# Batch-aligned token groups, merged transposes and merged stores in a pooled-attention and tanh-shrink kernel

## The chip, the cores and the metric

The kernel runs on one NeuronCore of one Trainium2 chip. The metric is the device time of one execution in microseconds (us), the median of several runs. The engines are named as in the profile: PE (TensorE, matmuls), PEld (its weight loads, which overlap PE), DVE (VectorE), ACT (ScalarE), POOL (GpSimd) and SP (SyncE, which here only issues DMAs). An instruction queue with a q behind its name (SPq) is the engine's sequencer. Matmul results go to PSUM, eight banks of 512 fp32 per partition; everything else that is on the core lies in SBUF, 128 partitions wide. A DMA moves data on up to 16 DMA engines.

## The reference: what is computed

Inputs are q, k and v of shape (8 batches, 8 heads, 576 tokens, 64), and two weights, w_in (512 x 2048) and w_out (2048 x 512). All are fp32.

```python
k_p = k.reshape(B, H, 72, 8, D).mean(axis=3)      # keys and values pooled by 8 tokens
v_p = v.reshape(B, H, 72, 8, D).mean(axis=3)
scores = scale * q @ k_p^T ; attn = softmax(scores)
attn_out = attn @ v_p                             # (8, 8, 576, 64)
x = attn_out.transpose(0, 2, 1, 3).reshape(4608, 512)
h = x @ w_in
out = (h - tanh(h)) @ w_out                       # (4608, 512)
```

## The kernel before

**Groups of tokens.** The second half (h, then the product with w_out) works on 9 groups of 512 tokens. A batch has 576 tokens, so in the kernel before group g holds tokens 512 g to 512 g + 511 of the running numbering, and its edges drift through the batches: group 1 is the last 64 tokens of batch 0 and 448 of batch 1, group 8 is the last 512 of batch 7. Within a batch the first 512 tokens are stored with token 4 p + j at partition p of block j (j = 0 to 3), so that one partition reads a contiguous stretch; the last 64 tokens (QT) form a short block.

**x.** Attention output is made in blocks of 128 tokens by av (L441): av_mms (L391) issues six matmuls for a block, whose weights are 128 columns of E (the exponentials) and which stream 130 columns of VB (the pooled values and a column for the denominator). DVE takes the reciprocal (rden, L433) and multiplies (x_sb, L434). The fifth block of a batch takes the last 128 tokens, S - 128 to S, of which 64 are used. x_sb then has to be transposed into xT, with features on partitions: by PE against an identity and an ACT copy for batches 0 and 1 (x0_turn L856, x_pe_transpose L468), by a DMA transpose on SP for batches 2 to 7 (x_dma_transpose L457). xT is one ring of 3 x 512 token columns; a block that crosses the ring's end takes two transposes. Blocks that the next group does not need are put on the list `late`, and their transposes are issued when the next group starts its products. x_sb has five buffers.

**One group** (loop at L964) has two stages. In the h stage, 64 matmuls of 512 columns (h_mms, L555) fill pairs of PSUM banks; ACT makes the tanh (TS, L570) and DVE the difference (Gt, L571). In the product stage, the multiplication with w_out is done as seven products of half matrices, 14 units of 8 x 2 matmuls of 256 columns (product, L610), with sums on DVE and copies on ACT in between (after_product, L652). The attention of batch g + 1 is threaded into the units of group g: scores (L359) at units 0 to 4, and av at units 6, 7, 8, 9 and 11. A score tile t of 0 to 3 holds one pair of heads; t = 4 holds what is left of all pairs, as four matmuls with 32-column weights each. Scores of batches 2 to 7 are computed in two halves of 288 columns, each with its own exponential on ACT; batches 0 and 1 use 512 columns and a joint tail of 64 (scores_wide L374, scores_tail L383). Groups 7 and 8 have no attention threaded in.

**Order of the work.** The schedule is written out by hand; each engine runs its instructions in program order, and the framework adds the semaphores. SP issues, per group: the k transpose of the next batch, five q transposes (L205), the loads of the batch after that (k, v, q), and the x transposes. POOL issues the stores of the group before (store_tile, L633) at the start of a group, then copies kT into KB (k_place), and pools k and v of a later batch in the product stage. PSUM banks are handed out in turn (Banks, L74).

**Group 0 and group 1's attention** stand before the loop: group 0's h and product are threaded with batch 1's attention (L921 to L959, units u = 0 to 15 of four matmuls each), with its k transpose at u = 2, q transposes at u = 3 to 5, av at u = 9 to 13 and the x transposes two units later.

**Stores.** out_segments (L484) cuts a tile of 128 tokens where it crosses a batch or a block, so a tile takes one to three DMAs. The last group is stored in halves of 256 columns as its products come out (store L628, called at L667, L668, L1020, and the loop at L1025), by SP, POOL and ACT. The issue lines are L631, L635 and L1026:

```python
for r0, r1, dst in out_segments(g * TG + th * HT + tt * 128, 128):
    engs[tt].dma_start(out=dst[:, c0:c1], in_=O[r0:r1, 2 * th + tt, c0:c1])
```

Of the kernel before, what the change touches and what calls it, by code (L numbers as in the profile page):

```python
# [19 lines left out]
NHP = H // 2  # L20
# [3 lines left out]
T = B * S  # L24
NFB = DM // 128
# [9 lines left out]
RING = 3 * TG  # L35
# [7 lines left out]
def kernel(  # L43
# [54 lines left out]
    xT = const.tile([128, NFB, RING], BF16, name="xT")  # L98
# [100 lines left out]
    def q_dma_transpose(b, j0=0, j1=R + 1):  # L199
        if j0 == 0:  # L200
            qTs[b] = work.tile([128, NHP, S], BF16, name="qT", tag="qT")
        qT = qTs[b]
        for j in range(j0, j1):
            rows = 128 if j < R else QT
            nc.sync.dma_start_transpose(  # L205
                out=qT[:, :, j * 128 : j * 128 + rows],
                in_=q_bf[:rows, j, :, :].rearrange("p h d -> p (h d)"),
            )

    def q_pe_transpose(b, hps, eng=None):  # L210
        if b not in qTs:
            qTs[b] = work.tile([128, NHP, S], BF16, name="qT", tag="qT")
        qT = qTs[b]
        for hp in hps:
            ps = ps_any([128, QA], FP32, "qT_ps")
            for j in range(R):
                nc.tensor.matmul(
                    ps[:, j * 128 : (j + 1) * 128],
                    lhsT=q_bf[:, j, 2 * hp : 2 * hp + 2, :].rearrange("p h d -> p (h d)"),
                    rhs=ident[:, :],  # L220
                    start=True,
                    stop=True,
                )
            evac(qT[:, hp, 0:QA], ps[:, :], eng)

    def q_pe_tail(b):
# [9 lines left out]
        evac(qTs[b][:, :, QA:S], ps[:, :, :])  # L236
# [109 lines left out]
    def score_mms(b, t, dst, c0, c1, pairs=range(NM)):  # L346
        for m in pairs if t == NM else (t,):
# [6 lines left out]
                rhs=qTs[b][:, m, c0:c1],  # L354
                start=True,
                stop=True,
            )

    def scores(b, t):  # L359
        if t == 0:  # L360
            E_tiles[b] = work.tile([128, NT, S], BF16, name="E", tag="E", bufs=1)
        E = E_tiles[b]
        hs = S // 2
        pss = []
        for half in range(2):
            ps = ps_b1([128, hs], FP32, "s_ps")
            score_mms(b, t, ps[:, :], half * hs, (half + 1) * hs)
            pss.append(ps)
        for half, ps in enumerate(pss):
            nc.scalar.activation(  # L370
                out=E[:, t, half * hs : (half + 1) * hs], in_=ps[:, :], func=ACT.Exp, scale=SCALE
            )

    def scores_wide(b, ts):  # L374
# [3 lines left out]
        for t in ts:  # L378
            ps = ps_any([128, QA], FP32, "s_ps")
            score_mms(b, t, ps[:, :], 0, QA)  # L380
            nc.scalar.activation(out=E[:, t, 0:QA], in_=ps[:, :], func=ACT.Exp, scale=SCALE)

    def scores_tail(b):  # L383
        ps = ps_any([128, NT, QT], FP32, "s_ps")
        for t in range(NT):
            score_mms(b, t, ps[:, t, :], QA, S)
# [4 lines left out]
    def av_mms(b, blk, half, ps):  # L391
        E = E_tiles[b]
        vb = VB[b % 2]
        c0 = blk * 128 if blk < 4 else S - 128
        for n in range(3):
# [6 lines left out]
                lhsT=E[:, t, c0 : c0 + 128],  # L402
# [7 lines left out]

    def av_half(b, blk, half, x_sb, alloc):
        ps = alloc([128, 4, D1], FP32, "x_ps")
        av_mms(b, blk, half, ps)
        rden = work.tile([128, 4, 1], FP32, name="rden", tag="rden", bufs=4)
        nc.vector.reciprocal(out=rden[:, :, :], in_=ps[:, :, D:D1])
# [3 lines left out]
            in1=rden[:, :, :].to_broadcast([128, 4, D]),  # L419
# [3 lines left out]
    def new_x():  # L423
        return work.tile([128, 2, 4, D], BF16, name="x_sb", tag="x_sb", bufs=5)

    def av_both(b, blk, x_sb):
        b0 = ps_a.ids[ps_a.n % len(ps_a.ids)]
        ps_a.n += 2
        ps = PS[:, b0 : b0 + 2, 0 : 4 * D1].rearrange("p k (h d) -> p k h d", d=D1)
        for half in range(2):  # L430
            av_mms(b, blk, half, ps[:, half, :, :])
        rden = work.tile([128, 2, 4, 1], FP32, name="rden2", tag="rden2")
        nc.vector.reciprocal(out=rden[:, :, :, :], in_=ps[:, :, :, D:D1])  # L433
# [3 lines left out]
            in1=rden[:, :, :, :].to_broadcast([128, 2, 4, D]),  # L437
# [3 lines left out]
    def av(b, blk, alloc, by_dma):  # L441
        x_sb = new_x()
        if by_dma:
# [4 lines left out]
        if by_dma:  # L448
            if b * S + blk * 128 < (b + 1) * TG:
                x_dma_transpose(b, blk, x_sb)  # L450
            else:
                late.append((b, blk, x_sb))
        return x_sb

    late = []

    def x_dma_transpose(b, blk, x_sb):  # L457
        p0 = 0 if blk < 4 else 64
        pos = (b * S + blk * 128) % RING
        p1 = min(128, p0 + RING - pos)  # L460
        for r0, r1, c in ((p0, p1, pos), (p1, 128, 0)):
            if r1 > r0:
                nc.sync.dma_start_transpose(
                    out=xT[:, :, c : c + r1 - r0],
                    in_=x_sb[r0:r1, :, :, :].rearrange("p a h d -> p (a h d)"),
                )

    def x_pe_transpose(b, blk, x_sb, fbs=(0, 4)):  # L468
        p0 = 0 if blk < 4 else 64
        pos = b * S + blk * 128  # L470
        f0, f1 = fbs
        xf = x_sb.rearrange("p a h d -> p (a h d)")
        ps = ps_any([128, f1 - f0, 128], FP32, "xT_ps")
        for fb in range(f0, f1):
            nc.tensor.matmul(
                ps[:, fb - f0, p0:128],
                lhsT=xf[:, fb * 128 : (fb + 1) * 128],
                rhs=ident[:, p0:128],
# [3 lines left out]
        nc.scalar.copy(out=xT[:, f0:f1, pos : pos + 128 - p0], in_=ps[:, :, p0:128])  # L482

    def out_segments(c0, nrows):  # L484
        segs = []
        r = 0
        while r < nrows:
            c = c0 + r
            bb = c // S
            i = c % S  # L490
            if i < QA:
                j = i // 128
                p0 = i % 128
                ln = min(128 - p0, nrows - r, QA - i)
                dst = out[bb * S : bb * S + QA, :].rearrange("(p j) m -> p j m", j=R)[
                    p0 : p0 + ln, j, :
                ]
            else:
                ln = min(S - i, nrows - r)
                dst = out[bb * S + i : bb * S + i + ln, :]  # L500
            segs.append((r, r + ln, dst))
            r += ln
        return segs
# [3 lines left out]
    def mlp_h_mms(g, i, f0, f1, pool=None):  # L507
        tok0 = g * TG
        if f0 == 0:
            h_tiles[i] = ps_h.tile([128, TG]) if pool is None else pool  # L510
        for fb in range(f0, f1):
# [3 lines left out]
                rhs=xT[:, fb, tok0 : tok0 + TG],  # L515
# [18 lines left out]
    def mlp_o(g, tb, i0, i1, gts, pool=None):  # L534
# [12 lines left out]
        if i1 == NHID:  # L547
# [4 lines left out]
            for r0, r1, dst in out_segments(g * TG + tb * 128, 128):  # L552
                nc.sync.dma_start(out=dst, in_=o_sb[r0:r1, :])

    def h_mms(g, i, dst):  # L555
        c0 = (g * TG) % RING
        for fb in range(NFB):
# [3 lines left out]
                rhs=xT[:, fb, c0 : c0 + TG],  # L561
# [66 lines left out]
    def store(g, th, engs, c0, c1):  # L628
        for tt in range(2):
            for r0, r1, dst in out_segments(g * TG + th * HT + tt * 128, 128):  # L630
                engs[tt].dma_start(out=dst[:, c0:c1], in_=O[r0:r1, 2 * th + tt, c0:c1])  # L631

    def store_tile(g, tb):  # L633
        for r0, r1, dst in out_segments(g * TG + tb * 128, 128):
            nc.gpsimd.dma_start(out=dst, in_=O[r0:r1, tb, :])  # L635
# [16 lines left out]
    def after_product(g, n):  # L652
# [11 lines left out]
        if n == 3:  # L664
            nc.vector.tensor_tensor(out=O[:, 0:2, HD:DM], in0=m4, in1=chain(g, C2), op=ALU.subtract)
            if g == NG - 1:
                store(g, 1, (nc.sync, nc.sync), 0, HD)  # L667
                store(g, 0, (nc.sync, nc.sync), HD, DM)  # L668
# [14 lines left out]
    zeros = xT[:, NFB - 1, RING - 512 : RING]  # L683
# [172 lines left out]
    def x0_turn(blks, half, b0, eng):  # L856
        n = len(blks)
        ps = bank(b0, [128, 2, n, 128])
        for i, blk in enumerate(blks):
# [8 lines left out]
        c = blks[0] * 128  # L868
        eng(
            out=xT[:, 2 * half : 2 * half + 2, c : c + n * 128],  # L870
            in_=ps.rearrange("p f i c -> p f (i c)"),
# [34 lines left out]
    for i in range(5, NHID):  # L906
# [5 lines left out]
        if i == 11:  # L912
            x4 = av(0, 4, ps_any, False)
        if i == 13:
            x_pe_transpose(0, 4, x4)
# [5 lines left out]
    for u in range(16):  # L921
        qd, tb = u // 4, u % 4
# [136 lines left out]
```

## Time and profile before

| what | value |
|---|---|
| median of 3 runs | 294.2 us (294.19 to 294.36) |
| the profiled execution's own time | 293.78 us |
| its span, first to last instruction | 292.1 us |
| granted TensorE clock | 0.997 |
| PE busy | 279.8 us (96% of the span) |
| DVE, ACT, POOL busy | 222.5, 153.4, 135.9 us |
| DMA moved | 49.84 MB, mean 171 GB/s |
| end of the last matmul | 286.4 us |

How to read it: times are from the start of the span. A row of a group of instructions names the line, the engine, the operation and what it writes and reads (out<-in). A row of waits says who waited for whom, and how long in total, how often, and at most. A stretch row gives its length, the busy time of PE, PEld, DVE, ACT and POOL with their numbers of instructions, the granted clock, the share of time that the 16 DMA engines were busy, and what they moved in GB/s. The chain that ended last is followed back from the last instruction; each piece has its start and its length. For a DMA the issue is on the issuing engine, and "to landing" runs from the issue until its semaphore tells that all data has arrived.

### The profile page before, as it was taken

How to read it: one execution, taken by the hardware profiler on the slowest of the kernel's cores; microseconds unless marked ns; L12 is line 12 of the kernel's file. 1: busy time of each engine (PE TensorE's matmuls, PEld its weight loads, DVE VectorE, ACT ScalarE, POOL GpSimd, SP SyncE). 2: the span in 40 equal slices, each digit the busy share in tenths (PEclk: the TensorE clock that was granted, in tenths of full speed). 3: DMA queues.
4: the chain of work that ended last, by engine and by line, in shares of the span. 5: the costliest groups of instructions: out<-in, count | busy, mean ns of one | idle time of the engine just before them, and what ended most of it. 6: DMA issues, size and time to landing. Idle time of an engine off the chain costs nothing.

```text
span 292.1 us, 5384 instructions
## 1 busy us (share of the span) xinstructions
PE 279.8 (96%) x2040; PEld 179.0 (61%) x2040; DVE 222.5 (76%) x348; ACT 153.4 (53%) x243; POOL 135.9 (47%) x160
## 2 busy tenths in 40 slices
PE   7999989999999998999999989999999999999992
PEld 3454445445874686458845874489448944874681
DVE  5659666689986996599859975998599849927971
ACT  4747586586438642765186516660866056225510
POOL 8600818990199429911994199408950040030001
PEclk9999999999999999999999999999999999999998
DMA  7999999938936999599959994998392360021023
GB/s 253 228 212 281 304 204 336 308 77 249 247 72 105 285 319 114 134 241 314 97 102 264 323 120 89 258 333 118 79 190 44 61 167 2 0 79 67 0 57 90
DMA packets 64810, 49.84 MB, mean 171 GB/s; under 512 B 40048, under 2 KB 53744, under 8 KB 64784
## 3 DMA queue, kind: packets, MB, share of 16 engines
q1 hardware_dynamic: 54816, 35.40, 51.6%
q0 software_dynamic: 7312, 12.19, 18.8%
q10 hardware_dynamic: 2656, 1.90, 2.3%
q8 instruction: 16, 0.26, 0.4%
q14 instruction: 10, 0.08, 0.1%
HBM read 36.70 MB, written 9.44 MB: 158 GB/s over the span
## 4 chain that ended last, share of the span: by engine, by line
PE 74%; DMA 12%; DVE 5%; POOL 4%; issue 1%; ACT 1%; SPq 0%; POOLq 0%; DVEq 0%; ACTq 0%
PE PS L558 34%; PE PS L614 29%; DMA w1b<-in_moe_w_in_dram 4%; PE PS L540 4%; DMA xT<-x_sb 4%; DMA k_raw<-in_k_dram 4%; PE PS L398 3%; PE PS L351 3%; DVE Gt L571 2%; POOL k_raw L248 1%; ACT q_bf L192 1%; DVE P L579 1%; DVE m L671 1%; POOL k_raw L255 1%; POOL kd L258 1%
## 5 line engine op out<-in xcount | busy, mean ns | idle before, releaser
L558 PE MATMUL PS<-xT,w1b 128*128 128x512 bf16 x512 | 111.8, 379 | 2.9 <-DVE rden L433 1.3
L571 DVE TENSOR_TENSOR Gt<-PS,TS 128x1024 bf16<-128x1024 f32 x56 | 68.3, 1220 | 31.2 <-ACT TS L570 31.2
L558 PEld LDWEIGHTS <-w1b 128*128 128x128 f16 x512 | 49.7, 98 | 62.4 <-issue 2.8
L570 ACT ACTIVATE TS<-PS 128x1024 f32<-128x1024 f32 x56 | 57.3, 1024 | 33.2 <-PE PS L558 29.2
L248 POOL TENSOR_TENSOR k_raw<-k_raw 128x512 f32<-128x512 f32 (+2 forms) x13 | 21.1, 1638 | 74.2 <-DVE rden L433 44.2
L635 POOL DMA_DIRECT2D out_dram<-O x44 | 23.7, 547 | 40.0 <-DVE O L673 22.3
L614 PE MATMUL PS<-w2s,Dg 128*128 128x256 f16 x256 | 30.2, 273 | 0.0
L614 PEld LDWEIGHTS <-Gt 128*128 128x128 bf16 x256 | 24.4, 98 | 5.6 <-DVE Gt L576 0.5
L614 PEld LDWEIGHTS <-P 128*128 128x128 bf16 x256 | 24.6, 98 | 4.7 <-issue 1.4
L614 PEld LDWEIGHTS <-Dg 128*128 128x128 bf16 x256 | 24.5, 98 | 2.6
L370 ACT ACTIVATE E<-PS 128x288 bf16<-128x288 f32 x60 | 21.4, 410 | 8.1 <-PE PS L351 7.8
L434 DVE TENSOR_TENSOR x_sb<-PS,rden 128x512 bf16<-128x512 f32 x30 | 20.7, 691 | 5.9 <-DMA xT<-x_sb 5.0
L579 DVE TENSOR_TENSOR P<-Gt 128x1024 bf16<-128x1024 bf16 x32 | 22.2, 694 | 0.6
L398 PE MATMUL PS<-VB,E 128*128 128x130 bf16 x240 | 20.2, 220 | 0.1
L670 ACT COPY m<-PS 128x512 f32<-128x512 f32 x8 | 4.7, 586 | 29.5 <-PE PS L614 29.5
L589 DVE TENSOR_TENSOR Dg<-Gt 128x1024 bf16<-128x1024 bf16 x32 | 19.9, 682 | 0.0
L269 POOL TENSOR_TENSOR v_raw<-v_raw 128x512 f32<-128x512 f32 (+1 forms) x12 | 19.7, 1657 | 0.0
L398 PEld LDWEIGHTS <-E 128*128 128x128 bf16 x240 | 16.8, 98 | 1.9 <-issue 0.4
L351 PE MATMUL PS<-qT,KB 128*128 128x288 bf16 (+5 forms) x128 | 17.0, 289 | 0.1
L1019 ACT COPY O<-PS 128x512 f32<-128x512 f32 x7 | 4.1, 585 | 24.5 <-PE PS L614 24.5
L614 PE MATMUL PS<-w2s,Gt 128*128 128x256 f16 x128 | 16.7, 273 | 0.2 <-DVE Gt L576 0.2
L614 PE MATMUL PS<-w2s,P 128*128 128x256 f16 x128 | 16.3, 273 | 0.0
(112 smaller groups left out, 389.6 us busy)
## 6 DMA issues: line engine op xcount, KB each, us to landing
k_raw<-in_k_dram SPq DMA_DIRECT2D x7, 1024.0 KB, 9.1
q_raw<-in_q_dram SPq DMA_DIRECT2D x7, 1024.0 KB, 11.3
v_raw<-in_v_dram SPq DMA_DIRECT2D x7, 1024.0 KB, 11.3
out_dram<-O POOLq DMA_DIRECT2D x32, 128.0 KB, 3.8
out_dram<-O POOLq DMA_DIRECT2D x12, 256.0 KB, 3.5
w1b<-in_moe_w_in_dram POOLq DMA_DIRECT2D x4, 512.0 KB, 13.9
w2b<-in_moe_w_out_dram POOLq DMA_DIRECT2D x4, 512.0 KB, 17.3
out_dram<-O SPq DMA_DIRECT2D x4, 256.0 KB, 4.6
```

What stands on the lines that cost most here:

```text
L248: first = eng.tensor_tensor(out=r[:, ta:tb, 0:4, :], in0=r[:, ta:tb, 0:4, :], in1=r[:, ta:tb, 4:8, :], op=ALU.add)
L351: nc.tensor.matmul(dst[p : p + w], lhsT=KB[b % 2][:, o : o + w], rhs=qTs[b][:, m, c0:c1], start=True, stop=True,)
L370: nc.scalar.activation(out=E[:, t, half * hs : (half + 1) * hs], in_=ps[:, :], func=ACT.Exp, scale=SCALE)
L398: nc.tensor.matmul(ps[:, 2 * n : 2 * n + 2, :].rearrange("p h d -> p (h d)") if n < 2 else ps.rearrange("p (a s) d -> p a s d", s=2)[:, :, ...
L434: nc.vector.tensor_tensor(out=x_sb[:, :, :, :], in0=ps[:, :, :, 0:D], in1=rden[:, :, :, :].to_broadcast([128, 2, 4, D]), op=ALU.mult,)
L558: nc.tensor.matmul(dst, lhsT=w1b[:, fb, i * 128 : (i + 1) * 128], rhs=xT[:, fb, c0 : c0 + TG], start=(fb == 0), stop=(fb == NFB - 1),)
L570: nc.scalar.activation(out=t2, in_=PS[:, b0 : b0 + 2, :], func=ACT.Tanh)
L571: nc.vector.tensor_sub(out=Gt[:, p, :, :], in0=PS[:, b0 : b0 + 2, :], in1=t2)
L579: nc.vector.tensor_tensor(out=P[:, a:b, :], in0=Gt[:, a:b, 0, :], in1=Gt[:, a:b, 1, :], op=ALU.add)
L589: return nc.vector.tensor_tensor(out=Dg[:, a:b, :, :], in0=Gt[:, a:b, :, 0:HT], in1=Gt[:, a:b, :, HT:TG], op=ALU.subtract,)
L614: nc.tensor.matmul(part(g, bk, tt), lhsT=lhs(k, slice(tt * 128, (tt + 1) * 128)), rhs=rhs[:, k, :], start=(first and k == 0 and (tt == 0 o ...
L635: nc.gpsimd.dma_start(out=dst, in_=O[r0:r1, tb, :])
```

## The change

Group g of 0 to 7 becomes the first 512 tokens of batch g, and group 8 becomes the last 64 tokens of all eight batches. What follows from it:

- x lies in 128-token blocks: two buffers xT[0] and xT[1] of four blocks, one for even and one for odd batches, and xT_last for group 8, whose tile t holds the tails of batches 2 t and 2 t + 1. h_mms streams x[:, :, fb, :], four runs of 128 columns.
- x_sb holds a pair of blocks, and one DMA transpose turns a pair (128 x 1024); the tail takes a third one of 64 rows. The transposes of blocks 2 and 3 are issued behind av of block 3. The list `late` goes. The tails of batches 0 and 1 are turned by DMA, not by PE.
- q is laid out alike: qT in blocks plus a separate tail qt, with three DMA transposes per batch instead of five.
- Scores of batches 2 to 7 use scores_wide and scores_tail; av moves one unit earlier, to units 5, 6, 7, 8 and 10. The fifth block computes 64 rows, with 64-column weights.
- Stores: one DMA per half group (two tiles); for group 8 one per tile, whose destination is two runs of 64 rows.
- In group 0's stage, k_transpose(1) moves from u = 2 to u = 3, and x_pe_transpose of block 3 goes ahead of unit 14. Group 1's h stage starts in banks 2 and 3 instead of 0 and 1.

The core of the diff:

```diff
-    xT = const.tile([128, NFB, RING], BF16, name="xT")
+    xT = [const.tile([128, 4, NFB, 128], BF16, name=f"xT{i}") for i in range(2)]
+    xT_last = const.tile([128, 4, NFB, 128], BF16, name="xT_last")
...
         else:
             nc.scalar.copy(out=q_bf[:QT, R, :, :], in_=q_raws.pop(b)[:QT, :, R, :])
 
-    def q_dma_transpose(b, j0=0, j1=R + 1):
-        if j0 == 0:
-            qTs[b] = work.tile([128, NHP, S], BF16, name="qT", tag="qT")
-        qT = qTs[b]
-        for j in range(j0, j1):
-            rows = 128 if j < R else QT
+    def q_tiles(b):
+        if b not in qTs:
+            qTs[b] = (
+                work.tile([128, R, NHP, 128], BF16, name="qT", tag="qT"),
+                work.tile([128, NHP, QT], BF16, name="qt", tag="qt"),
+            )
+        return qTs[b]
+
+    def q_dma_transpose(b, n):
+        qT, qt = q_tiles(b)
+        if n < 2:
             nc.sync.dma_start_transpose(
-                out=qT[:, :, j * 128 : j * 128 + rows],
-                in_=q_bf[:rows, j, :, :].rearrange("p h d -> p (h d)"),
+                out=qT[:, 2 * n : 2 * n + 2, :, :].rearrange("p j h c -> p (j h) c"),
+                in_=q_bf[:, 2 * n : 2 * n + 2, :, :].rearrange("p j h d -> p (j h d)"),
+            )
+        else:
+            nc.sync.dma_start_transpose(
+                out=qt[:, :, :], in_=q_bf[:QT, R, :, :].rearrange("p h d -> p (h d)")
             )
...
-                rhs=qTs[b][:, m, c0:c1],
+                rhs=qTs[b][1][:, m, :] if tail else qTs[b][0][:, :, m, :],
...
-        c0 = blk * 128 if blk < 4 else S - 128
+        c0 = blk * 128
+        c1 = min(S, c0 + 128)
...
-                lhsT=E[:, t, c0 : c0 + 128],
+                lhsT=E[:, t, c0:c1],
...
+    x_pairs = {}
+
+    def x_block(b, blk):
+        if blk == 4:
+            x_pairs[b, 2] = work.tile([128, 2, 4, D], BF16, name="x_end", tag="x_end", bufs=1)
+            return x_pairs[b, 2][0:QT]
+        if blk % 2 == 0:
+            x_pairs[b, blk // 2] = work.tile([128, 2, 2, 4, D], BF16, name="x_sb", tag="x_sb")
+        return x_pairs[b, blk // 2][:, blk % 2]
...
+    def x_dma_transpose(b, n):
+        if n < 2:
+            nc.sync.dma_start_transpose(
+                out=xT[b % 2][:, 2 * n : 2 * n + 2, :, :].rearrange("p k f c -> p (k f) c"),
+                in_=x_pairs.pop((b, n)).rearrange("p k a h d -> p (k a h d)"),
+            )
+        else:
+            c = (b % 2) * QT
+            nc.sync.dma_start_transpose(
+                out=xT_last[:, b // 2, :, c : c + QT],
+                in_=x_pairs.pop((b, 2))[0:QT].rearrange("p a h d -> p (a h d)"),
+            )
...
+    def out_part(g, t0, t1, c0=0, c1=DM):
+        if g < NB:
+            v = out[g * S : g * S + QA, :].rearrange("(p j) m -> p j m", j=R)
+            return v[:, t0:t1, c0:c1]
+        v = out.rearrange("(t k s) m -> k s t m", k=2, s=S)
+        return v[:, QA:S, t0:t1, c0:c1]
...
+        x = xT[g % 2] if g < NB else xT_last
...
-                rhs=xT[:, fb, c0 : c0 + TG],
+                rhs=x[:, :, fb, :],
...
-    def store(g, th, engs, c0, c1):
-        for tt in range(2):
-            for r0, r1, dst in out_segments(g * TG + th * HT + tt * 128, 128):
-                engs[tt].dma_start(out=dst[:, c0:c1], in_=O[r0:r1, 2 * th + tt, c0:c1])
-
-    def store_tile(g, tb):
-        for r0, r1, dst in out_segments(g * TG + tb * 128, 128):
-            nc.gpsimd.dma_start(out=dst, in_=O[r0:r1, tb, :])
+    def store(g, t0, t1, eng, c0=0, c1=DM):
+        n = t1 - t0 if g < NB else 1
+        for t in range(t0, t1, n):
+            eng.dma_start(out=out_part(g, t, t + n, c0, c1), in_=O[:, t : t + n, c0:c1])
...
-                store(g, 1, (nc.sync, nc.sync), 0, HD)
-                store(g, 0, (nc.sync, nc.sync), HD, DM)
+                store(g, 2, 4, nc.sync, 0, HD)
+                store(g, 0, 2, nc.sync, HD, DM)
...
             load_q(2)
-        if u == 2:
+        if u == 3:
             k_transpose(1, ps_any, (nc.vector.tensor_copy, nc.vector.tensor_copy))
-        if u == 3:
             q_pe_transpose(1, (0, 1), "act")
...
+        if u == 14:
+            x_pe_transpose(1, *pend.pop(0))
...
-            h_pair(g, p, (0, 2, 4, 6, 0, 2, 4)[p], p % 2)
+            h_pair(g, p, ((2, 0, 4, 6, 0, 2, 4) if g == 1 else (0, 2, 4, 6, 0, 2, 4))[p], p % 2)
...
-                for tb in (2, 3, 0, 1):
-                    store_tile(g - 1, tb)
+                store(g - 1, 2, 4, nc.gpsimd)
+                store(g - 1, 0, 2, nc.gpsimd)
...
-        while late:
-            x_dma_transpose(*late.pop(0))
...
-                    scores(nb, u)
+                    scores_wide(nb, (u,))
                 if u == NT:
-                    ps_a.n += 2
-                if u in (6, 7, 8, 9, 11):
-                    av(nb, (6, 7, 8, 9, 11).index(u), ps_b1, True)
+                    scores_tail(nb)
+                if u in (5, 6, 7, 8, 10):
+                    blk = (5, 6, 7, 8, 10).index(u)
+                    av(nb, blk, ps_b1, True)
+                    if blk in (1, 3, 4):
+                        x_dma_transpose(nb, blk // 2)
...
-    store(NG - 1, 1, (nc.sync, nc.gpsimd), HD, DM)
+    store(NG - 1, 2, 4, nc.sync, HD, DM)
     bk, lhs, rhs = products[6]
-    for tt, eng in ((0, nc.scalar.copy), (1, nc.vector.tensor_copy)):
+    for tt, copy, eng in ((0, nc.scalar.copy, nc.scalar), (1, nc.vector.tensor_copy, nc.sync)):
         product(NG - 1, bk, lhs, rhs, 0, NP, False, (tt,))
-        eng(out=O[:, tt, 0:HD], in_=part(NG - 1, C1, tt))
-        for n, (r0, r1, dst) in enumerate(out_segments((NG - 1) * TG + tt * 128, 128)):
-            (nc.scalar if tt == 0 or n else nc.sync).dma_start(
-                out=dst[:, 0:HD], in_=O[r0:r1, tt, 0:HD]
-            )
+        copy(out=O[:, tt, 0:HD], in_=part(NG - 1, C1, tt))
+        store(NG - 1, tt, tt + 1, eng, 0, HD)
```

## The prediction

> **What bounds the kernel now.** I read the page first: its span, and how busy each engine is.
>
> ```profile
> span 292.1 us, 5384 instructions
> PE 279.8 (96%) x2040; PEld 179.0 (61%) x2040; DVE 222.5 (76%) x348; ACT 153.4 (53%) x243; POOL 135.9 (47%) x160
> ```
>
> PE works for 279.8 of 292.1 us, so a gain can only be fewer PE instructions, one of the few PE waits, or the 5.7 us behind the last matmul (it ends at 286.4). The waits on PE, with columns for total, times and longest us, are these:
>
> ```profile
> PE PS L558 <- DVE rden L433: 1.3, 1, 1.3
> PE PS L558 <- DMA xT<-x_sb: 1.0, 1, 1.0
> PE PS L312 <- POOL kd L258: 0.8, 1, 0.8
> PE PS L558 <- DVE O L549: 0.7, 1, 0.7
> ```
>
> Next come stretches of one group each: the product stages of groups 2, 4, 6 and 7 (length, then PE busy time).
>
> ```profile
> 99.37:115.77 16.40, 15.41 (x158) 13.30 (x157) 13.83 (x25) 6.77 (x16) 8.07 (x6) 1.00 1.18 252
> 158.97:175.64 16.67, 15.40 (x159) 13.27 (x158) 14.14 (x25) 7.05 (x16) 8.34 (x6) 1.00 0.98 230
> 218.83:234.24 15.41, 15.41 (x159) 13.46 (x158) 13.62 (x25) 5.82 (x14) 0.86 (x2) 1.00 0.31 60
> 248.05:260.31 12.26, 12.26 (x113) 10.82 (x112) 9.50 (x15) 2.35 (x4) 0.72 (x2) 1.00 0.01 1
> ```
>
> Groups 2 and 4 lose 1.0 and 1.3 us at their ends, waiting for x; group 6 loses nothing. Group 7, without attention, shows that scores and AV of a batch cost 15.41 - 12.26 = 3.15 us of PE. Pieces of the chain that ended last (start, length) price the small steps:
>
> ```profile
> 45.17 0.70 PE PS L351 x12
> 46.83 0.35 PE PS L398 x6
> 85.48 13.89 PE PS L558 x64
> 112.34 3.29 DMA xT<-x_sb
> ```
>
> Last I read the transposes (time on SP, and under them time to landing, first for x, then for k) and the end: the issues of the last stores, and three stretches whose last two numbers are the busy share of the 16 DMA engines and GB/s.
>
> ```profile
> L463 SPq DMA_TRANSPOSE xT<-x_sb x31: 1187/1222/3519, 80.2 to 233.7; - x31
> DMA to landing us min/median/max: 2.3/3.9/9.9
> L334 SPq DMA_TRANSPOSE kT<-kd x6: 1198/1202/1605, 55.9 to 204.4; - x6
> DMA to landing us min/median/max: 2.6/3.0/4.3
> ...
> 278.61 7.89 SPq L631 DMA_DIRECT2D out_dram<-O  x10
> 286.92 0.47 SPq L1026 DMA_DIRECT2D out_dram<-O  x1
> ...
> 44.00:50.00 6.00, 6.00 (x54) 3.33 (x53) 3.55 (x12) 3.90 (x7) 4.88 (x5) 1.00 0.96 345
> 260.90:264.00 3.10, 3.10 (x16) 1.37 (x14) 0.87 (x1) 1.26 (x3) 1.43 (x3) 1.00 0.90 300
> 279.80:289.40 9.60, 6.59 (x61) 5.65 (x58) 4.28 (x7) 1.18 (x3) 1.06 (x2) 1.00 0.45 112
> ```
>
> GB/s over 16 times the share is the rate of one busy DMA engine: 22.5 GB/s for loads in a stream, 20.8 for a stream of stores, 15.6 for the scattered last stores. A row of 1 KB takes one engine 46, 49 and 66 ns.
>
> **The change, part by part.** The profiled execution took 293.78 us, its span and 1.7 around it; the median shown is 294.2, so I add the sum's change to that.
>
> *Scores.* Today's 3.15 us hold five AV blocks of 0.35, leaving 1.40 for scores. New are four 512-wide matmuls at 13.81/64 = 0.216 us, 0.86, plus what the chain shows as x12 (the leftover heads 512 wide and the eight 64-wide tails of batch 1), 0.70: 1.56, or 1.65 if the way into the 32-column matmuls is not in the 0.70. That adds 0.2 us for each of batches 2 to 7: **+1.2 us**. ACT does six exponentials instead of ten per batch, under PE; if the last were late, AV of block 0, now a unit earlier, still has one product unit and the tail scores (0.87 + 0.37 us) to cover one of about 0.6.
>
> *AV of the last block.* Its weights are now 64 columns wide. No row has such a matmul. Below, it costs what 128 columns do, 0. Above, it costs what the 32-column ones do: their group starts 0.1 us late and the next full matmul 0.1 us late, 0.2. I take 0.2, as those are the only narrow rows: 7 batches behind the pinned point below, **+1.4 us** (0 to 1.4).
>
> *Waits that go.* Both x waits come from the old buffers: a block's x_sb waited for the transpose of five blocks before it (DVE L434 on the transposes, 5.0 us in all), and rden queued behind it on DVE. Two pair buffers are free long before. **-2.3 us.** What is late next is the pair transpose.
>
> *Stage of groups 0 and 1.* k_transpose(1) starts at 37.62, pinned by POOL. One o unit (4 x 0.216 = 0.86) moves ahead of it, into a wait that was 0.8; q's copy to SBUF then ends 0.2 us late for the first score: -0.65 (0 if q's cast also waits). The x_pe_transpose(0, 4) that goes lies before that point and gains nothing. Group 1 no longer starts in the bank that waits for the last O copy (-0.7), and four 64-wide transposes go (-0.1): **-1.45 us** (-0.7 to -1.6).
>
> *Pair transposes.* Now blocks 2 and 3 are both due at the group's start, for every batch from 2. A clean 512-column transpose lands in 2.45 us, a 640-column one (kT) in 2.6; 1024 columns then make 3.05. Above stands two in a row, 1.2 + 2.45 = 3.7, or 4.9 if all of it doubles. DVE ends m4 about 8.0 us into the product stage (group 6: 226.78 - 218.83), then four blocks of rden and x_sb at 0.86 and one O of 0.61: the pair goes to SP at 12.1. PE ends the stage at 12.26 + 1.56 + 1.75 + 0.2 = 15.8. That leaves 3.7 us, so no wait in a quiet queue. Group 1 has two more w_sum steps of 0.6 on DVE ahead of it, so about 0.6 wait; groups 2 to 5 have the loads of the next batch in front, now issued about 1 us earlier since q has three transposes instead of five: 0.1 each. **+1.0 us** (0.2 to 3).
>
> *Moved DMAs.* The batch 0 tail on SP stands before load_k(2), which waits for w2 until 42 us anyway; the batch 1 tail delays q's transposes by 1.2 us, and they are due some 10 us later. On POOL, 2 store issues for 5 to 8 of 0.55 us bring k_place forward; nothing waits for that.
>
> So far: 1.2 + 1.4 - 2.3 - 1.45 + 1.0 = -0.15 us.
>
> *The last stores.* Old group 8 is written by 16 transfers of 64 rows, 1 KB each; every one names its rows in one run. The new ones are 8 transfers of 128 rows, 64 from each of two batches, so the destination counts 2, then 64, then 256 elements. How the chip deals such a transfer over its engines, no row shows. Below: over all 16, 8 rows each, as today. Above: cut at the outermost count, which gives 2 engines 64 rows each. Then all 8 transfers lie on the same two engines, 512 rows each, at 46 to 66 ns: 23.6 to 33.8 us. I take 55 ns, between the streams and today's stores: 28.2 us. The first packets move 1.2 us after the first issue, at 279.8; the last then leave at 308.0, not 289.4, and PE has long stopped. With 0.5 us to land and 1.5 for the closing waits the span ends near 310.0: **+17.9 us**. I take the upper end, since every transfer that is seen to spread counts 16 (the small v loads), 64 or 128 at its outermost step on both sides; none counts 2.
>
> The Trainium skill, "DMA: Bandwidth & Descriptors", section "Why a DMA increments its semaphore by 16 and not by 1", says that a transfer uses the largest number of engines up to 16 that divides the slowest dimension of both its sides. By that rule 2 engines write each of these stores, and the sum is 311.9; without it the sum is 292.5.
>
> **Sum:** 294.2 - 0.15 + 17.9 = 311.9 us.
>
> **The rivals.**
> *The stores spread over 16 engines.* For it: today's 128 KB stores on POOL land in 3.8 us, and all of today's rows spread. Then the end gets shorter: POOL has no store left there (it drains until 291.3 now, 1 us after SP is through), and ACT issues one store instead of three. The last landing moves from 289.9 to about 289.2 and the end to 290.5, -1.5. Time: 294.2 - 0.15 - 1.5 = 292.5 us (291 to 295), faster. It decides from the point where the last store takes under 3.5 us to land.
> *The pair transposes cost double,* 4.9 us: 4.9 + 0.1 - 3.7 = 1.3 us of PE wait at six group starts, 0.6 more at group 2's, against the 1.0 counted: +7.4. Against it: kT, a quarter wider, takes no longer on SP. With the slow stores the PE delay moves the first store too: 319; with spread stores 300.
> *The slow stores overlap more than I think:* at 46 ns, and with a short close, 306.5; at 66 ns 318.
>
> **How the numbers follow.** Forecast (two engines, transposes in time) 0.72; double transposes with it 0.08; spread stores 0.17; spread stores with late transposes 0.03. The range covers the forecast from 46 to 66 ns a row, with 2 us for the body, and double transposes at its upper edge: 304 to 319. What it leaves out is the 0.2 of spread stores. About 0.2% can be told from no change here. Slower 0.72 + 0.08 + 0.03 = 0.83; the spread case is faster in 0.14 and same in 0.03.
>
> **What will show it.** Right: PE ends within 2 us of 286 while the span is about 310; the last 20 us have a DMA share near 2/16 = 0.13 at some 40 GB/s; the stores of group 8 land 5 to 25 us after issue, the later the longer. The waits on kd, the O copy and rden are gone, one of about 0.6 on xT stands at group 2, and L351 has 512- and 64-wide forms. Wrong: the last stores land in 2 to 3 us (then 292.5 follows), PE waits over 1 us for xT at every group, or the 64-column AV costs nothing.

## The result, and the profile after

The changed kernel takes 306.31 us (median of 4 runs, 306.05 to 307.19), the kernel before 294.19 us on the same chip: 1.0418 times as long, 95% interval 1.0394 to 1.0441. Ratios given with an interval leave out the runs that fell in a slower state of the chip, so they can differ a little from the quotient of the medians. The profiled execution took 306.07 us, its span and 1.7 us around it. From its page, the span, PE's busy time, the granted clock and the DMA engines' busy share over the span:

```profile
span 304.4 us, 5228 instructions
PE 282.4 (93%) x2031; PEld 177.9 (58%) x2032; DVE 219.4 (72%) x348; ACT 151.3 (50%) x217; POOL 117.7 (39%) x128
...
PEclk9999999999999999999999999999999999999955
DMA  7999999989258955995599479947304200300111
```

PE is busy 2.6 us longer than before, and POOL works 18 us less, which buys nothing that shows. The new thing is at the right: in the last three slices (23 us) the DMA engines are a tenth busy. In the last two PE does nothing, and the clock row falls there too. Two stretches of that end (start and end, length, busy times of the five engines, clock, DMA share, GB/s):

```profile
280.50:302.50 22.00, 6.59 (x61) 5.67 (x58) 4.28 (x7) 1.18 (x3) 0.00 (x0) 0.72 0.14 47
288.00:302.00 14.00, 0.00 (x0) 0.00 (x0) 0.00 (x0) 0.00 (x0) 0.00 (x0) 0.58 0.14 48
```

And the issues of group 8's stores on SP (ns min/median/max, first and last start), then the last two of them (start, length, together):

```profile
L613 SPq DMA_DIRECT2D out_dram<-O x7: 506/670/3767, 279.3 to 291.3; - x7
...
287.40 7.64 SPq L613 DMA_DIRECT2D out_dram<-O  x2
```

For 22 us the share stands at 0.14, little more than 2/16 = 0.125, at 47 to 48 GB/s, while for 14 of them no engine computes. The trace's 1 KB packets of the stores number 1024, the first at 280.58, the last done at 303.11: 512 rows for each of two engines in 22.5 us, 44.0 ns a row. The last two issues on SP took 3.77 us each; the trace doesn't say what they waited for. The packets of the first store end 4.7 us after its issue, those of the last 11.8 us after; the prediction had 5 to 25 us to landing.

Next the chain that ended last (start, length, what), ahead of group 2's start and in its product stage (L392 is av_mms), and then, of the waits on PE (total, times, longest), the only one on a transpose of x and a new one on the copy of kT:

```profile
83.26 3.05 DMA xT<-x_sb
...
107.22 0.45 PE PS L392 x6
...
108.54 0.35 PE PS L392 x6
...
113.08 0.47 PE PS L392 x6
```

```profile
PE PS L225 <- DVE KB L311: 0.7, 1, 0.7
PE PS L540 <- DMA xT<-x_sb: 0.5, 1, 0.5
```

A pair transpose lands in 3.05 us. It holds PE up once, at group 2, by 0.5 us. Of a batch's five AV blocks, the first, behind the narrow score matmuls, and the last, with 64-column weights, take 0.45 and 0.47 us, the others 0.35.

Where the time came from, by the starts of the h stages in the two traces:

| | before | after | difference |
|---|---|---|---|
| group 1 starts | 55.51 | 55.11 | -0.40 |
| group 1's length | 29.87 | 31.33 | +1.46 |
| group 2 | 30.39 | 29.66 | -0.73 |
| group 4 | 30.65 | 29.67 | -0.98 |
| groups 3, 5, 6 | 29.22 each | 29.66 each | +1.34 together |
| group 7's length | 26.08 | 26.08 | 0 |
| last matmul ends | 286.39 | 287.09 | +0.70 |
| from there to the end of the span | 5.68 | 17.27 | +11.59 |

The body is as good as unchanged: waits that went pay for the products of another shape. The end of the stores makes the loss.

### The profile page after: what moved, and what is told of

It reads as the page before. It is cut to its first block, busy times and chain, and to the rows that moved or that the text cites. A ratio compares the mean times of both kernels' runs of the same rounds, so it can differ in the third digit from the quotient of the medians.

```text
span 304.4 us, 5228 instructions
## 1 busy us (share of the span) xinstructions
PE 282.4 (93%) x2031; PEld 177.9 (58%) x2032; DVE 219.4 (72%) x348; ACT 151.3 (50%) x217; POOL 117.7 (39%) x128
## 4 chain that ended last, share of the span: by engine, by line
PE 82%; DVE 7%; DMA 3%; ACT 1%; issue 1%; SPq 0%; ACTq 0%; DVEq 0%
PE PS L540 32%; PE PS L596 31%; PE PS L392 5%; PE PS L523 5%; PE PS L359 4%; PE PS L495 3%; DVE Gt L553 3%; DMA k_raw<-in_k_dram 2%; DVE Gt L508 1%; DMA xT<-x_sb 1%; DVE w2s L579 1%; DVE P L561 1%; PE PS L778 0%; PE PS L689 0%; PE PS L225 0%
## 5 line engine op out<-in xcount | busy, mean ns | idle before, releaser
L540 PE MATMUL PS<-xT,w1b 128*128 128x512 bf16 x448 | 98.0, 379 | 0.6 <-DMA xT<-x_sb 0.5
L552 ACT ACTIVATE TS<-PS 128x1024 f32<-128x1024 f32 x56 | 57.3, 1024 | 31.1 <-PE PS L540 27.5
L374 ACT ACTIVATE E<-PS 128x512 bf16<-128x512 f32 x40 | 23.7, 598 | 12.3 <-PE PS L359 12.2
L613 POOL DMA_DIRECT2D out_dram<-O x14 | 7.8, 557 | 46.9 <-DVE O L651 44.7
L392 PE MATMUL PS<-VB,E 128*128 128x130 bf16 (+1 forms) x240 | 20.4, 221 | 0.1
L392 PEld LDWEIGHTS <-E 128*128 128x128 bf16 (+1 forms) x240 | 15.9, 100 | 3.4 <-issue 1.6
L430 DVE TENSOR_TENSOR x_sb<-PS,rden 128x512 bf16<-128x512 f32 x24 | 16.6, 691 | 0.8
L596 PE MATMUL PS<-w2b,Gt 128*128 128x256 f16 x128 | 16.3, 273 | 0.0
L596 PE MATMUL PS<-w2s,Q 128*128 128x256 f16 x128 | 16.3, 273 | 0.0
```

Of the source, the lines that this page charges most:

```text
L392: nc.tensor.matmul(ps[:, 2 * n : 2 * n + 2, :].rearrange("p h d -> p (h d)") if n < 2 else ps.rearrange("p (a s) d -> p a s d", s=2)[:, :, ...
L430: nc.vector.tensor_tensor(out=x_sb[:, :, :, :], in0=ps[:, :, :, 0:D], in1=rden[0:n, :, :, :].to_broadcast([n, 2, 4, D]), op=ALU.mult,)
L540: nc.tensor.matmul(dst, lhsT=w1b[:, fb, i * 128 : (i + 1) * 128], rhs=x[:, :, fb, :], start=(fb == 0), stop=(fb == NFB - 1),)
L552: nc.scalar.activation(out=t2, in_=PS[:, b0 : b0 + 2, :], func=ACT.Tanh)
L596: nc.tensor.matmul(part(g, bk, tt), lhsT=lhs(k, slice(tt * 128, (tt + 1) * 128)), rhs=rhs[:, k, :], start=(first and k == 0 and (tt == 0 o ...
```

## The experiments

The theory: group 8's stores lie on two DMA engines because their destination counts 2 outermost. Rivals: the rows' address pattern (runs of 64 rows in two batches) or their number makes them slow; or the end is late for another reason in the body. Kernels E1 to E4 stood beside a kernel before of 294.57 us, E5 to E8 beside 294.32, E9 and E10 beside 294.15.

**E1: each store of group 8 in two.** The same rows go to the same addresses, in transfers of 64 rows.

```diff
+        if g == NB:
+            for t in range(t0, t1):
+                for k in range(2):
+                    r = (2 * t + k) * S
+                    eng.dma_start(
+                        out=out[r + QA : r + S, c0:c1],
+                        in_=O[k * QT : (k + 1) * QT, t, c0:c1],
+                    )
+            return
```

> The changed kernel with each store of group 8 split into two of 64 rows, one per batch, on the same queues: the same rows and bytes, twice the issues. Theory (a store whose destination counts 2 at its outermost step is written by 2 DMA engines): each store has 16 engines again. SP then issues ten stores of about 0.55 us from 283.1 on and the last two wait for the final copy, so the last lands near 291 and the span ends 1.2 later, at 292.2; time 293.9 us (293 to 294.6), 12.4 less than the changed kernel. Rival A (the two far-apart runs of rows in HBM are slow to write): the same rows are written, so the last 20 us stay, about 305. Rival B (fewer, larger stores hold one queue up): also faster, like the theory; the interleaved kernel tells them apart.

294.9 us, 1.0008 times the kernel before (0.9982 to 1.0035). The stores' issues and their landings, on the line of that loop:

```profile
L615 SPq DMA_DIRECT2D out_dram<-O x14: 466/594/1543, 279.7 to 290.1; - x14
...
DMA to landing us min/median/max: 2.0/2.1/3.4
```

From the last matmul (287.50) to the end of the span (293.05) it is 5.55 us, against 17.27. So the shape of the transfers is the whole loss. Twice as many issues cost nothing that shows here; without the slow stores the change is worth nothing either way.

**E2: the eight stores kept, but counted another way.** The tokens of a tile of group 8 alternate between its two batches, so that the destination counts 64 outermost and then 2. For that, group 8's h matmuls read xT_last in steps of 64 columns.

```diff
-        v = out.rearrange("(t k s) m -> k s t m", k=2, s=S)
-        return v[:, QA:S, t0:t1, c0:c1]
+        v = out.rearrange("(t k s) m -> s k t m", k=2, s=S)
+        return v[QA:S, :, t0:t1, c0:c1]
...
+            x = xT_last.rearrange("p t f (k s) -> p t f s k", k=2)
```

> The changed kernel with the tokens of each tile of group 8 taken in another order: row s of the one batch, then row s of the other. The destination of a store then counts 64, 2, 256 instead of 2, 64, 256: still one store per tile, the same 128 rows, the same two batches, the same queues, the same 8 issues. For this the 64 h matmuls of group 8 read x in steps of 64 columns, whose price on PE no row shows (0 to 13.8 us for these 64; it is read from PE's stretch and taken off). Theory: 16 engines, the last store lands near 290, the span ends at 291.1, time 292.8 us plus that price. Rivals A and B: nothing about the rows, the bytes or the number of stores has changed, so the time stays near 306.

309.94 us (1.0482 to 1.0557 times before). It loses its time for quite another reason, as two of the chain's last pieces say (group 8's h stage and its products):

```profile
261.02 30.93 PE PS L542 x64
291.94 12.24 PE PS L598 x112
```

The stores land in 2.1 to 3.8 us, and the end behind the last matmul (304.17) is 3.50 us, shorter than in any other kernel here: with the same number of stores, the same rows and the same sizes, the outermost count decides. But the 64 matmuls of group 8's h stage took 30.93 us, not 13.8: 0.483 us each instead of 0.216. I had bounded that step's price at 13.8; it was 17.1, and 309.94 - 17.1 = 292.8 is the time expected without it.

**E3: four outermost.** A tile holds 32 tokens of four batches; for this the tails are transposed in two halves.

```diff
+        v = out.rearrange("(t k s) m -> k s t m", k=4, s=S)
+        r = QA + 32 * (t0 % 2)
+        return v[:, r : r + 32, t0 // 2, c0:c1]
```

> The changed kernel with tiles of group 8 made of 32 tokens from each of four batches: the destination of a store counts 4, 32, 256 (the tails are transposed in two halves for it). Theory: 4 engines, 32 rows of 44 ns = 1.4 us each per store; the first four stores are through by 287.1, the last four run from 287.3 to 292.9, the span ends at 294.1 and the time is 295.8 us (295 to 297.5); the DMA share in the last microseconds is near 4/16. Rival A: four far runs instead of two, as slow as the changed kernel or slower (306 or more). Rival B: the same 8 stores, 306.

296.88 us (1.0057 to 1.0124). From the last matmul to the end it is 7.84 us, between the 17.27 with two and the 5.55 of E1. The stretch of its stores:

```profile
280.00:294.50 14.50, 7.20 (x66) 6.20 (x64) 4.90 (x8) 1.54 (x3) 0.00 (x0) 0.83 0.23 73
```

A share of 0.23 is close to 4/16. The DMA packets from 278 us on say the same: among them, beside the 1024 rows, are 4-byte packets that follow the rows of each store (the count under 512 B). The changed kernel first, then E3, then E2, each with eight such stores:

```profile
DMA packets 1041, 1.07 MB, mean 36 GB/s; under 512 B 16, under 2 KB 1040, under 8 KB 1040
```

```profile
DMA packets 1057, 1.07 MB, mean 36 GB/s; under 512 B 32, under 2 KB 1056, under 8 KB 1056
```

```profile
DMA packets 1153, 1.07 MB, mean 36 GB/s; under 512 B 128, under 2 KB 1152, under 8 KB 1152
```

That is 2, 4 and 16 for a store; E1 has 256 for sixteen stores, again 16. If every engine at work ends its part of a store with one, which the shares bear out, outermost counts of 2, 4 and 64 give 2, 4 and 16 engines. The Trainium skill, "DMA: Bandwidth & Descriptors", section "Why a DMA increments its semaphore by 16 and not by 1", has just that rule, the largest number of engines up to 16 that divides the slowest dimension of both sides, and the traces agree at 2 (share 0.14), at 4 (0.23) and, by the 4-byte packets, at 64.

**E4 and E5: the narrow matmuls.** E4 is E1 with 128-column weights in the fifth AV block, as before (c0 = S - 128 for block 4, its last 64 rows transposed). E5 is E1 with the two groups of narrow score matmuls next to each other:

```diff
+    def scores_end(b):
...
+        for t in range(NM):
+            score_mms(b, t, pt[:, t, :], True)
+        score_mms(b, NM, pw[:, :], False)
+        score_mms(b, NM, pt[:, NM, :], True)
```

> The split stores, and the fifth AV block with 128-column weights again (the last 128 tokens of the batch, of which 64 are used), instead of 64-column ones. Theory (64-column matmuls cost a switch of the array on the way in and out, 0.23 us a batch): 6 to 7 batches, 1.4 to 1.6 us less than the split stores alone, about 292.4 us. Rival (the 0.12 before and 0.11 behind them are weight loads that any matmul on E pays there): no difference within 0.3 us.

> The split stores, and for batches 2 to 7 the 32-column score matmuls of the last tile set next to each other: 64-wide tails of the four full tiles first, then the 32-column ones, 512 wide and 64 wide, in one unit. The array goes into the narrow form and out of it once per batch instead of twice. Theory: 0.2 us for each of six batches, 1.2 us less than the split stores (294.9), 293.7. Rival (the excess is in the 64-wide matmuls themselves, or the later exponential of the first part then holds AV up): no gain within 0.3 us, or a loss.

E4 took 293.37 us (0.9948 to 0.9988 of before), E5 293.70 us (0.9941 to 0.9997). Pieces of the chain in one group, the fifth AV block and the products behind it, first of E1, then of E4:

```profile
143.15 0.46 PE PS L392 x6
143.61 2.73 PE PS L596 x24
```

```profile
142.93 0.35 PE PS L392 x6
143.28 2.62 PE PS L596 x24
```

The block and the products behind it are 0.11 us shorter each: 0.22 us for going into 64-column weights and out again, as the prediction took from the 32-column rows. Over seven batches that is 1.5, and 294.90 - 293.37 = 1.53. In E5 the score pieces and the first AV block take 0.48 and 0.35 us where E1 has 0.33, 0.26 and 0.46: again 0.22 a batch, so each change of the weights' width costs 0.1 us here and there were two too many.

**E6: k's transpose in another PSUM bank.** The wait on KB is that of q's second transpose, at 39.11 us. The banks there are handed out in turn, and one o unit ahead of k_transpose(1) gives that transpose the bank of k's result, which DVE has not copied yet. E6 is E1 with k_transpose(1) in bank 1.

> The split stores, and k_transpose(1) at u = 3 writes its four tiles into PSUM bank 1, which nothing uses then, instead of the next of the three banks. Theory (the second q transpose waits 0.74 us for the copies of KB, because it gets k's bank): the wait goes; the first score then waits for q's copy until about 39.9 instead of starting at 40.6, so 0.5 us less than the split stores, 294.4. Rival (ACT's q copies end the wait anyway): no difference within 0.2 us.

294.27 us (0.9983 to 1.0028); E1 had 294.90 beside the other kernel before, 1.0008 times it. The wait on KB is gone, and another of 0.7 us stands in the same stage, that of group 0's products (L523) on the load of w2b. Group 1 starts no earlier (55.55 against 55.36) and is no shorter (31.85 against 31.49), though that trace is of a run of 295.36 us, near the slowest of the twelve. A gain is not shown.

**E7 and E8: is there a faster version?** E8 is the change with group 8's stores cut by batch of a tile instead of by tile, so that one transfer takes the 64 rows of both tiles (ten stores in all):

```diff
+        if g == NB:
+            v = out.rearrange("(t k s) m -> k s t m", k=2, s=S)
+            for k in range(2):
+                eng.dma_start(
+                    out=v[k, QA:S, t0:t1, c0:c1], in_=O[k * QT : (k + 1) * QT, t0:t1, c0:c1]
+                )
+            return
```

E7 is E8 with the edits of E4, E5 and E6.

> The changed kernel with the stores of group 8 cut by batch half instead of by tile: one store for the first (or second) 64 partitions of both tiles of a half group, so its destination counts 64, 2, 256; still 128 rows each. Theory (the outermost count sets the number of engines): 16 engines, and with ten stores instead of the sixteen of the split stores SP is through earlier: the last store lands near 290.2, the span ends at 291.4, time 293.1 us, about 1 less than the split stores. Rival (it is the short stores of 64 rows in one run that make it fast): each store writes rows of two batches and two tiles, so it stays at 306.

> The stores cut by batch half, 128-column weights in the fifth AV block, joint narrow scores and the free bank for k together. Theories as above: 293.1 - 1.5 - 1.2 - 0.5 = 289.9 us, 4.4 less than the kernel before (290 to 291). If the terms don't add up (each gain covered by a wait for x or for ACT), 291.5 to 293.

E8 took 293.47 us (0.9959 to 1.0006): its end behind the last matmul is 4.43 us against E1's 5.55. E7 took 292.13 us, 0.9922 times the kernel before (0.9897 to 0.9947). It beats both kernels, the changed one by 14 us, but falls short of the 290 to 291 expected. Groups 2 to 6 are 29.22 to 29.57 us, where 29.22 is the undisturbed length before. Group 1 is 31.76 us. It starts at 54.53, 0.8 us earlier than E1's, and yet group 2 starts at 86.29, much as in E1 (86.85) and in the changed kernel (86.44). What holds group 1 is DVE, whose work in its h stage lies on the chain without a break: four sums of 16-bit weights (L590) between the Gt steps, of uneven length (1.39, 0.55, 0.99 and 0.41 us on the chain), while POOL pools v and places it beside them.

**E9: without POOL's adds.** E7, with the three adds of pool_v(2) on POOL left out.

> Edit: the kernel with all four edits together, with the three adds on POOL that pool v of batch 2 left out (so batch 2's values are wrong; the multiplications by the mask and everything else stay). Theory that POOL's adds slow DVE's sums of 16-bit weights beside them: in group 1's h stage the four sums of two rows of w_out's blocks, on the chain with 1.39, 0.55, 0.99 and 0.41 us, all take about 0.41 (the shortest); DVE is then 1.7 us earlier at the end of the h stage, group 1 shortens from 31.8 to about 30.2 us, the rest of the kernel stays as it is: 290.6 us (from 292.1). Rival that these sums are slow for a reason of their own (the first touch of their data, the wait for PSUM or ACT): the sums keep their durations, group 1 stays at 31.8 and the time at 292.1.

290.79 us, 0.9888 times before (0.9852 to 0.9924). The second and third of the four sums (start, length): first in E7, each under the POOL operation that runs when it starts, then in E9, where none runs then:

```profile
59.98 1.61 POOL L280 TENSOR_TENSOR v_raw<-v_raw 128x640 f32<-128x640 f32 x1
61.24 0.62 DVE L590 TENSOR_TENSOR w2s<-w2b 128x512 f16<-128x512 f16 x1
...
62.67 1.04 POOL L291 TENSOR_TENSOR VB<-v_raw,mask 128x512 bf16<-128x512 f32 x1
62.93 1.07 DVE L590 TENSOR_TENSOR w2s<-w2b 128x512 f16<-128x512 f16 x1
```

```profile
60.45 0.41 DVE L591 TENSOR_TENSOR w2s<-w2b 128x512 f16<-128x512 f16 x1
...
62.30 0.42 DVE L591 TENSOR_TENSOR w2s<-w2b 128x512 f16<-128x512 f16 x1
```

With nothing on POOL beside them they take 0.41 us, and so does the fourth; the first went from 1.47 to 0.75 and still has a POOL operation beside it. The lengths follow a pattern: in E7 the second sum ends 0.27 us after the POOL add beside it (61.59), the third 0.29 us after the multiplication (63.71). In the twelve traces of this case, 41 of the 42 such sums that started while a POOL operation ran ended 0.27 to 0.30 us after its end, however early they started (the other one started 0.05 us before that end and took 0.42 us), and the six that started beside none took 0.41 to 0.42 us. So it isn't the adds alone, and what a sum costs depends on the moment at which it meets POOL. Group 1 is 30.50 us instead of 31.76, and group 2 starts at 84.90. That accounts for the 1.3 us (292.13 - 290.79); next on the chain there, until 61.16, is ACT with the tanhs and q's casts. The Trainium skill, "SBUF — State Buffer", section "SBUF: two separate sides", says why that may be: DVE with two SBUF inputs and GpSimd lock one pair of ports against each other for whole instructions. The traces agree in that a sum ends only behind the POOL operation that runs when it starts; the lock itself they don't show. E9 is no version to keep, since it leaves out work; it says what moving that work would be worth.

**E10: is it any step, or a long one?** The changed kernel, where group 8's h matmuls read even tokens first, then odd ones (its rows come out in that order).

```diff
+            x = xT_last.rearrange("p t f (s k) -> p t f k s", k=2)
```

> Edit: the changed kernel, where group 8's h matmuls read the 128 tokens of each tile as even tokens first, then odd ones: steps of two columns (4 bytes) instead of 64 (the rows of group 8 so come out in another order, which is left that way; nothing is done less). Theory that any step in the moving operand slows a matmul: 0.48 us instead of 0.216 for each of the 64, group 8's h stage 30.9 us instead of 13.8, the time 323.4 us. Rival that only long steps do (128 bytes were slow): 0.216 us each and 306.3 us. In between (some 0.3 us each, 312) the price grows with the step.

307.62 us in one run, and the 64 matmuls in the chain:

```profile
262.06 14.45 PE PS L542 x64
```

0.226 us each: a step of 4 bytes costs next to nothing, one of 128 bytes 0.27 us a matmul. The other 1 us of the time lies in group 1 (32.35 us against 31.33), far from the edit: there the first of the four sums starts 0.03 us into a POOL add and takes 2.06 us, against 1.04 in the changed kernel. The Trainium skill, "SBUF — State Buffer", section "Door 1: The DMA port swizzle (why `[64,N]` ≈ `[32,N]`)", says that SBUF has lines of 16 bytes and that every access that crosses to a new line pays; by that a 4-byte step is free and a 128-byte one is not, and the runs agree, but for the 0.01 us of the 4-byte step. Steps between the two were not run.

## Why the prediction was right, and where not

The forecast was 311.9 us with a range of 304 to 319; it is 306.31. The likeliest case is the one that came: two DMA engines, PE done by 287, a share near 0.13. E1, E2 and E3 show its mechanism. The terms of the sum were less good than the whole, and some of their errors cancel by luck:

- *Last stores, +17.9: measured +11.6.* This is the term that was mis-sized, by 6.3 us. The body came out 0.85 us above its forecast, so the miss of the whole is 5.6 (0.2 of it lies between the medians and the profiled runs). A row took 44.0 ns, not 55; I chose the middle between the loads of a stream (46) and today's scattered stores (66). It lies just under the low end. 512 rows make 22.5 us instead of 28.2 (-5.7). Landing and closing took 1.25 us (303.11 to 304.36), not 2.0 (-0.7). The first packet moved at 280.58, not 279.8 (+0.8), since PE ends 0.70 us later than before. Why the rows were as quick as those of a stream stays open. It isn't that only two engines have them: the median row packet took 46 ns in the changed kernel, but also in E2 on 16 engines, and in E3 and E10; in the kernel before, E1 and E4 to E9 it took 69 to 71. The first four write a store from all 128 partitions, the others from 64; whether that is the reason was not tried.
- *Scores +1.2 and AV +1.4: right.* An undisturbed group is 0.44 us longer (29.66 against 29.22) where the forecast had 0.2 + 0.2. E4 and E5 measured the two at 0.22 each. The chain pieces of 0.35 and 0.70 were enough to price a width that no row showed.
- *Waits that go, -2.3: right,* about -2.6: over the undisturbed 29.22, groups 2 and 4 had 1.17 and 1.43 us, and nothing of it is left.
- *Pair transposes, +1.0: +0.5.* 3.05 us to land, as worked out; 0.5 us of wait at group 2, as worked out (0.6); the 0.1 us at each of groups 3 to 6 did not come. The rival of doubled transposes is refuted by the same row.
- *Stage of groups 0 and 1, -1.45: wrong, it measured +0.16.* Group 1 starts 0.40 us earlier, and its own length grows by 0.56 us beyond what is counted above (31.33 - 29.66 - 0.46 = 1.21 us over an undisturbed group, against 29.87 - 29.22 = 0.65). The step that failed is the -0.65: I placed one o unit (four matmuls of group 0's products) ahead of k_transpose(1) and asked only whether q's copy would be late, not which bank the next transposes would get. k_transpose(1) starts at 37.69 (37.62 before), and the wait on kd in front of it is gone with the o unit that fills it (-0.87). But a wait of 0.74 on KB, for a PSUM bank, and one of 0.21 on the copy of an earlier x transpose came. The O copy's wait (-0.67) and the 64-wide transposes (-0.1) went as forecast, the 64-column AV of batch 1 costs its 0.22 here: -0.87 + 0.74 + 0.21 - 0.67 - 0.1 + 0.22 + 0.07 (the later start) = -0.40, the measured gain. And that gain could not be kept, since PE paces the h stage of group 1 in neither kernel. Before, ACT (tanhs with q's casts between them) lies on the chain until 62.28 and DVE behind it; in the changed kernel DVE lies on it from 58.15 on. The last Gt halves (L576 before, L558 after) start at 70.93 us in the trace before and at 70.97 after, although the stage starts 0.4 us earlier. The four sums of E9 account for it: they started at other moments of POOL's work and took 1.04, 0.63, 1.06 and 0.48 us, against 0.41, 0.41, 0.68 and 0.48 before, 1.2 us more. The forecast has no term for that.
- *Body, -0.15 in all: +0.70.* That stage misses by 1.6; the waits and the pair transposes came out 0.8 better than forecast and hide half of it, which is luck.

The rival of spread stores (292.5, chance 0.17) is what E8 gives, 293.47, by an edit of the transfers alone. That it ended a microsecond higher is mostly the body: its last matmul ends at 286.74, where the sum has 286.25. The other rivals, 46 ns (306.5) and 66 ns a row, were ends of the forecast's own range; the lower one was nearly met.

Open in part: why the two engines reach 44.0 ns a row where E3's took 51 (256 rows for each of four, 280.72 to 293.80). Its trace has no row under way for 0.45 us of that stretch, which is 1.7 of the 7 ns. The rest is single packets that took longer (median 46 ns, mean 51.7, the longest 393), for which no cause is shown.

## What to carry to other kernels

Look at the outermost count of a DMA before merging transfers (here the destination's was varied): two transfers of 64 rows can be faster than one of 2 x 64. Cutting them otherwise (E1, E8) cost nothing that shows; ordering them otherwise (E2) cost 17.1 us, because PE's operand got a long step. The merge that saved instructions on POOL's queue bought nothing here, and the merged stores were paid for where nothing covers them, at the kernel's end. When a wait is removed in front of a stage, look first who paces that stage; here it was ACT and DVE, and PE's earlier start was lost. And look at which moment DVE's sums meet POOL's work: with a start 0.4 us earlier the four sums here came out 1.2 us longer.

## What the runs showed of the hardware

- 1 KB rows to DRAM over two DMA engines (a store whose destination counts 2 outermost): 44.0 ns a row and engine, 47 to 48 GB/s in all; the last two issues of such stores held SP for 3.77 us each.
- A moving operand read in steps of 128 bytes: 0.483 us for a matmul of 512 columns, against 0.216 in one piece or in runs of 128 columns and 0.226 in steps of 4 bytes.
- A change of the weights' width (128 to 64 or 32 columns, or back) cost about 0.1 us of PE.
- A 1024-column DMA transpose of 16-bit data landed in 3.05 us and held SP for 1.25 us (median of 12).
- A sum of 16-bit data on DVE, 0.41 us alone, ended 0.27 to 0.30 us after the POOL operation that ran when it started, and so took up to 2.06 us (E10).
- The median packet of a 1 KB row took 46 ns in stores that read 128 partitions and 69 to 71 ns in stores that read 64; why was not tried.
